# Scores and gathers one step further ahead in a talking-heads attention kernel, with a fourth gather buffer, against a first batch loaded all at once

## Chip, core and metric

One core of a Trainium2 chip runs the whole program in one launch. The metric is the device time of that launch in microseconds: 2410.34 us as the median of three runs (2408.38 to 2414.39). Everything is computed in 32-bit floats.

Five engines work beside each other, each in its own program order: TensorE (in the profile PE, and PEld for its weight loads), VectorE (DVE), ScalarE (ACT), GpSimd (POOL) and SyncE (SP). SyncE only issues transfers here, GpSimd issues some and computes, ScalarE issues transfers only at the start.

## What is computed

```python
# q, k, v: (8, 12, 448, 64); w_pre, w_post: (12, 12)
scores = (1 / sqrt(64)) * q @ k.T                      # per batch and head
scores = einsum('bhij,hg->bgij', scores, w_pre)        # heads are mixed before ...
attn = softmax(scores, axis=-1)                        # (with 1e-9 in the sum)
attn = einsum('bhij,hg->bgij', attn, w_post)           # ... and after the softmax
x = (attn @ v) as (8, 448, 768)
u = x + real(fft(fft(x, axis=1), axis=2))
un = (u - mean) / sqrt(var + 1e-6)
out = u + relu(un @ w_ch1) @ w_ch2                     # w_ch1: 768 x 3072, w_ch2: 3072 x 768
```

## The kernel before

**Attention** runs in 192 steps, 24 to a batch (`GS`), three to a block of score rows (`BS`), six to a group (`GT`). For a block, `emit_qk` computes the scores of all twelve heads (three pairs of pairs, `xx`) and ScalarE copies them from PSUM to `Sb`. Mixing heads is a matmul over heads, so heads have to lie in partitions: `emit_gather` moves a step's rows of `Sb` into `Kr`, with four transfers from SyncE. Then come, each for one step: premix (matmul by `w_pre`), maximum (VectorE), exponential (ScalarE), scaling (GpSimd), postmix (matmul by `w_post`), and a transpose on VectorE (`emit_turn`) that brings keys into partitions for attention times V (`emit_av`).

```python
    pkr = pool("pkr", 3)
    ppp = pool("ppp", 3)
    psm = pool("psm", 4)
    ...
    def emit_qk(n, xx):
        bk = blocks[n]
        st = batches[bk["b"]]
        if "Sb" not in bk:
            bk["Sb"] = psb.tile([P, 6, S], F32, name="Sb", tag="Sb")
        ...                                  # 16 matmuls into two PSUM tiles
        return [lambda x=x: copy(ENG["QK"][x], bk["Sb"][:124, 2 * xx + x, :],
                                 pss[x][:124, :S]) for x in range(2)]

    def emit_gather(T):
        Kr = pkr.tile([P, 2, S], F32, name="Kr", tag="Kr")
        Sb = blocks[T // BS]["Sb"]
        row = _row(Sb)
        for z in range(2):
            for x in range(2):
                p0 = MG + 4 * (T % BS) + 2 * z + x
                nc.sync.dma_start(
                    out=Kr[64 * x:64 * x + KR, z, :],
                    in_=_ap(Sb, p0 * row, [[RS * row, 2 * R], [S, 6], [1, S]]))
        steps[T]["Kr"] = Kr
    ...
        def done(y):                         # of emit_av
            for e in range(2):
                ...
                copy(ENG["AV"][y], dst, src)     # XT <- PSUM, 128 x 60
```

The order of work in a step is a list, one for even and one for odd steps; what is due in which step stands in tables. `LG` is how many steps a gather stands ahead of its postmix, `LM` how many the premix.

```python
AT_QK = ((1, 2, 2), (0, 1, 2), (0, 1, 2), (1, 1, 2),
         (0, 1, 2), (0, 1, 2), (0, 1, 2), (0, 1, 2))
ORDERS = tuple(o.split() for o in (
    "conv pre post flush AV max0 exp0 "
    "QK max1 exp1 turn scale full gather",
    "pre post flush max0 max1 QK exp0 "
    "AV turn exp1 scale gather conv full flush"))
    ...
    LG, LM = 4, 2
    ...
        for n in range(0 if b else 2, 2 * NG):
            for xx in range(3):
                due("QK", f + BS * n - 7 + AT_QK[n][xx],
                    lambda n=2 * NG * b + n, xx=xx: (emit_qk(n, xx), n))
    ...
        while s <= TOT - GS + AT_X[-1]:
            ...
            for op in ORDERS[s % 2]:
                if op == "flush":
                    flush()                  # pending copies out of PSUM
                elif op in fill:
                    take(op, s)              # what is due: QK, AV, transposes, Z, S2
                elif op == "conv":
                    if s >= 4:
                        wts.deal(1)          # one VectorE operation of the weights
                elif op == "gather":
                    if 0 <= s + LG < TOT:
                        if any(e[2] is not None and e[2] <= (s + LG) // BS for e in pend):
                            flush()
                        emit_gather(s + LG)
                ...                          # pre, max, exp, scale for s + LM; post, turn for s
```

**The first batch** has a path of its own: its q and k are all loaded at once, on SyncE and ScalarE, the last pair into a buffer of `Pv` that is free then; the scores of its first two blocks follow at once. All other batches load on GpSimd, step by step, into four raw buffers.

```python
        if y == 0 and b == 0 and xx == START[-1]:
            if "raw" not in first:
                first["raw"] = ppv.tile([P, GT, 2 * S], F32, name="Pv", tag="Pv")
            ...
            eng = nc.gpsimd if b else (nc.sync, nc.scalar)[x]
```

**Weights** come as 64-bit floats. VectorE turns every piece into 32 bits in seven operations (`begin` to `whole`), and four sums of pieces are formed besides, so that the network's products need fewer matmuls. `deal` hands out these operations, one a step in attention, two to four at a time in the network. Each piece and each sum is stored to memory from GpSimd; each has a buffer of its own (`slot`) but for the sum that goes onto piece 6.

```python
        def new(slot):
            box[slot] = self.pst.tile([P, DH], F32, name="wst", tag=f"wst{slot}")[:, :w]
            return box[slot]
        def store(slot):
            self.later.append(lambda: nc.gpsimd.dma_start(out=dst[slot], in_=box[slot]))
        ...
        def total(o, a, op, b):
            to = box[o] if o == 6 else new(o)
            vec.tensor_tensor(to, box[a], box[b], op=op)
            store(o)
```

**The network** (`ffn_phase`) follows: 42 rounds of seven products with `w_ch1` and seven with `w_ch2`, on TensorE nearly without a gap.

## Time and profile before

| stage | from, to (us) | PE busy | DVE busy | ACT busy | POOL busy |
|---|---|---|---|---|---|
| start, to the first turned step | 0 to 41.8 | 23.89 | 11.16 | 15.50 | 9.38 |
| attention, 100 us of it | 200 to 300 | 99.71 | 86.81 | 71.61 | 78.72 |
| attention, 100 us of it | 500 to 600 | 95.74 | 87.40 | 67.69 | 73.24 |
| passage to the network | 800 to 860 | 53.33 | 39.71 | 29.84 | 33.93 |
| network, 500 us of it | 1300 to 1800 | 500.00 | 281.32 | 57.58 | 60.26 |

The span is 2408.6 us with 54664 instructions. How the lines of a profile are read: a group has its line of the kernel, engine, operation, what it writes and reads, and a count; then busy time in us, mean ns of one, and the idle time of the engine just before it with what ended it. A wait reads "engine line <- who ended it: us in total, times, longest". A row of windows gives, after the length, busy us and count of each engine, then the granted clock of TensorE as a share of full speed, the busy share of the transfer engines, and GB/s. Starts of matmuls are recorded; their ends are modelled, so busy time of PE is more than its work.

### The profile page before, as it was taken

To read this page: it belongs to the slowest core of one execution; us is meant where nothing else is said; L and a number is where in the kernel's file an instruction comes from. 1 tells how busy PE (TensorE), PEld (TensorE's weight loads), DVE (VectorE), ACT (ScalarE), POOL (GpSimd) and SP (SyncE) were. 2 spreads that over 40 slices of the span, in tenths; PEclk is the share of its full clock that TensorE was granted. 3 is DMA by queue.
4 is the path that set the end of the run, shared out by engine and by line. 5 is a ranking of instruction groups with operands and counts; after the bars stand their busy time and mean duration, and the time that the engine had idled before them with its cause. 6 is when DMAs were issued, how large, how long until landed. Compare 5 with 4: busy or idle time off the path is not lost.

```text
span 2408.6 us, 54664 instructions
## 1 busy us (share of the span) xinstructions
PE 2361.9 (98%) x21680; PEld 1596.2 (66%) x21680; DVE 1543.8 (64%) x3139; ACT 798.8 (33%) x2055; POOL 787.3 (33%) x1255
## 2 busy tenths in 40 slices
PE   6999999999999999999999999999999999999999
PEld 2555555555555577677777777777777777777776
DVE  3888988888897767775656356635664457433333
ACT  4776777666667632221110110110110110111110
POOL 3597877868776541211111011101110011000000
PEclk9999999999999999999999999999999999999999
DMA  7565555655554566437444444544442644353331
GB/s 161 161 182 165 185 171 165 193 161 178 170 171 157 165 237 191 154 116 254 136 146 139 151 151 125 158 132 156 143 157 93 197 135 140 120 170 113 117 118 53
DMA packets 169100, 372.50 MB, mean 155 GB/s; under 512 B 36750, under 2 KB 90790, under 8 KB 168846
## 3 DMA queue, kind: packets, MB, share of 16 engines
q1 hardware_dynamic: 129902, 261.60, 33.1%
q0 software_dynamic: 33376, 106.03, 15.3%
q8 instruction: 173, 2.83, 0.5%
q10 hardware_dynamic: 5568, 1.38, 0.4%
q14 instruction: 81, 0.66, 0.1%
HBM read 211.98 MB, written 74.34 MB: 119 GB/s over the span
## 4 chain that ended last, share of the span: by engine, by line
PE 91%; DMA 3%; DVE 2%; ACT 1%; SPq 1%; POOL 1%; issue 1%; ACTq 0%; DVEq 0%; POOLq 0%
PE psP L980 18%; PE psP L1036 18%; PE psR L980 9%; PE psR L1036 9%; PE mx L486 7%; PE ms L459 5%; PE ms L547 5%; PE po L520 5%; PE psQ L1036 5%; PE psQ L980 5%; DMA Kr<-Sb 2%; PE ms L661 2%; PE ms L434 1%; PE ms L645 1%; SPq L475 1%; PE ms L580 1%
## 5 line engine op out<-in xcount | busy, mean ns | idle before, releaser
L980 PE MATMUL psP<-ub,w1t 128*128 128x256 f32 x2016 | 462.5, 379 | 0.0
L1036 PE MATMUL psP<-w2t,h 128*128 128x384 f32 x1344 | 460.9, 486 | 0.0
L980 PEld LDWEIGHTS psP<-ub,w1t 128*128 128x128 f32 x2016 | 382.8, 190 | 60.7
L213 POOL DMA_DIRECT2D raw<-in_moe_w_ch_dram x120 | 68.6, 571 | 919.4 <-DVE tmp L257 908.5
L1036 PEld LDWEIGHTS psP<-w2t,h 128*128 128x128 f32 x1344 | 254.4, 190 | 165.9
L510 POOL TENSOR_SCALAR PP<-PP,rcp 128x448 f32<-128x448 f32 x384 | 253.6, 670 | 228.2 <-DVE rcp L508 199.3
L500 ACT ACTIVATE PP<-mx,nmx 128x448 f32<-128x448 f32 x384 | 240.7, 632 | 172.3 <-DVE nmx L493 158.5
L493 DVE TENSOR_REDUCE nmx<-mx 128x1 f32<-128x448 f32 x384 | 222.7, 616 | 94.1 <-PE mx L486 91.9
L985 ACT COPY h<-psP 128x512 f32<-128x512 f32 x42 | 24.6, 586 | 764.7 <-PE psP L980 753.6
L1042 DVE TENSOR_TENSOR u<-u,psP 128x384 f32<-128x384 f32 x336 | 183.4, 552 | 141.4 <-PE psP L1036 139.2
L486 PE MATMUL mx<-Kr,kw 60*32 60x448 f32 x3072 | 236.4, 552 | 16.7 <-DMA Kr<-Sb 11.7
L980 PE MATMUL psR<-ub,w1t 128*128 128x256 f32 x1008 | 231.3, 379 | 0.0
L1036 PE MATMUL psR<-w2t,h 128*128 128x384 f32 x672 | 230.5, 486 | 0.0
L991 DVE TENSOR_TENSOR h<-h,psQ 128x512 f32<-128x512 f32 x42 | 28.9, 688 | 298.8 <-PE psQ L980 298.8
L520 PE MATMUL po<-PP,kw 60*32 60x448 f32 x3072 | 215.5, 541 | 4.9 <-DVE rcp L507 2.4
L531 DVE STREAM_TRANSPOSE Pv<-po 128x896 f32<-128x896 f32 x192 | 212.4, 1106 | 9.3 <-PE po L520 6.2
L459 PE MATMUL ms<-kT,qT 64*32 64x448 f32 (+1 forms) x3072 | 207.6, 545 | 7.4 <-ACT qT L330 6.4
L980 PEld LDWEIGHTS psR<-ub,w1t 128*128 128x128 f32 x1008 | 191.4, 190 | 25.9
L330 ACT COPY Sb<-ms 124x448 f32<-124x448 f32 x384 | 184.0, 542 | 33.8 <-DMA Kr<-Sb 17.4
L547 PEld LDWEIGHTS ms<-Pv,vv 64*64 64x64 f32 x5376 | 145.4, 134 | 70.5 <-issue 35.2
L1036 PEld LDWEIGHTS psR<-w2t,h 128*128 128x128 f32 x672 | 127.2, 190 | 87.4
L547 PE MATMUL ms<-Pv,vv 64*64 64x120 f32 x5376 | 168.6, 270 | 1.2 <-issue 1.2
(95 smaller groups left out, 2813.9 us busy)
## 6 DMA issues: line engine op xcount, KB each, us to landing
ub<-ub SPq DMA_DIRECT2D x294, 384.0 KB
Kr<-Sb SPq DMA_DIRECT2D x768, 105.0 KB
raw<-in_moe_w_ch_dram POOLq DMA_DIRECT2D x72, 256.0 KB, 3.6
raw<-in_moe_w_ch_dram POOLq DMA_DIRECT2D x48, 384.0 KB, 3.6
w<-wst POOLq DMA_DIRECT2D x126, 128.0 KB, 3.3
w<-wst POOLq DMA_DIRECT2D x84, 192.0 KB, 2.6
w1t<-w SPq DMA_DIRECT2D x42, 384.0 KB
w2t<-w SPq DMA_DIRECT2D x42, 384.0 KB
```

Of the source, the lines that this page charges most:

```text
L330: (nc.scalar.copy if eng == "a" else nc.vector.tensor_copy)(out=out, in_=in_)
L459: nc.tensor.matmul(pss[x][o:o + hi - lo, :S], st["qT", xx][64 * x:64 * x + 64, y, lo:hi], st["kT", xx][64 * x:64 * x + 64, y, :], start=Tr ...
L486: nc.tensor.matmul(mx[x][64 * z + o:64 * z + o + 32, :S], kw1[64 * x:64 * x + KR, o:o + 32], Kr[64 * x:64 * x + KR, z, :], start=True, sto ...
L493: nc.vector.tensor_reduce(nmx[:, :], steps[T]["mx"][x][:, :S], axis=AX.X, op=ALU.max, negate=True)
L500: nc.scalar.activation(steps[T]["PP"][:, x, :], steps[T]["mx"][x][:, :S], ACTF.Exp, bias=steps[T]["nmx", x][:, :], accum_out=steps[T]["den ...
L510: nc.gpsimd.tensor_scalar(PP[:, x, :], PP[:, x, :], rcp[:, x:x + 1], 1.0, op0=ALU.mult, op1=ALU.mult)
L520: nc.tensor.matmul(po[o:o + 32, z, :S], kw2[64 * z:64 * z + KR, y, :], PP[64 * z:64 * z + KR, :, c * HS:(c + 1) * HS], start=True, stop=True)
L531: nc.vector.transpose(g["Pv"][:, T % GT, :].rearrange("p (z s) -> p z s", z=2), steps[T]["po"][:, :, :S])
L547: nc.tensor.matmul(pss[y][64 * x:64 * x + 64, :nu * R], st["v", pr][64 * y:64 * y + 64, x, jb * D:(jb + 1) * D], _ap(Pv, 64 * y * rp + 32 ...
L980: nc.tensor.matmul(p[:, m, :], w1[i][:, kc, m * P:(m + 1) * P], ub[:, kc, :], start=i in OPENS and m == kc == 0, stop=kc == NK - 1, skip_g ...
L1036: nc.tensor.matmul(p, lhs[i][:, kf, x * P:(x + 1) * P], w2[i][:, kf, :], start=i in OPENS and kf == 0, stop=kf == FM - 1, skip_group_check ...
L1042: nc.vector.tensor_tensor(us_, us_, p, op=ALU.add)
```

## The change

What it does, in the order of weight:
- Scores and gathers go one step further ahead (`LG` 4 to 5, scores at −8 in place of −7), with a fourth buffer for `Kr`. It is for the premix to find its rows landed.
- To make room, `psm` has three buffers in place of four, `XT` is two columns narrower, and the weights' sums are written over pieces that are no longer needed, so that five staging buffers do in place of seven.
- The tables of what is due when, the two orders in a step and the choice of engine for some copies are new: half the copies of attention times V go to VectorE, and the smaller copy of k goes from VectorE to ScalarE.
- The first batch's own path is gone: its loads, transposes and scores follow the same tables as those of the other batches.

```diff

-XW = GR + 12
+XW = GR + 10
 ...
-AT_T = ((6, 10), (17, 18), (14, 16))
+AT_T = ((4, 11), (17, 16), (14, 14))
 AT_L = ((-4, -3), (-2, -1), (0, 1), (2, 8), (12, 13), (14, 15))
 AT_V = ((3, 4), (5, 6), (7, 7))
-AT_QK = ((1, 2, 2), (0, 1, 2), (0, 1, 2), (1, 1, 2),
-         (0, 1, 2), (0, 1, 2), (0, 1, 2), (0, 1, 2))
-AT_AV = ((1, 2, 3), (0, 1, 5), (3, 4, 5), (1, 2, 4))
-AT_X = (11, 20, 24, 29)
-AT_Z = (39, 39, 41, 41)
+AT_QK = ((0, 2, 3), (0, 1, 2), (1, 2, 3), (1, 1, 2),
+         (0, 1, 2), (0, 1, 2), (0, 0, 2), (0, 0, 2))
+AT_AV = ((1, 2, 3), (0, 1, 5), (3, 4, 5), (1, 3, 5))
+AT_X = (11, 20, 24, 30)
+AT_Z = (39, 39, 41, 42)
 AT_S = ((40, 44), (48, 54))
 
 ORDERS = tuple(o.split() for o in (
-    "conv pre post flush AV max0 exp0 "
-    "QK max1 exp1 turn scale full gather",
-    "pre post flush max0 max1 QK exp0 "
-    "AV turn exp1 scale gather conv full flush"))
+    "pre post max0 max1 exp0 AV QK "
+    "gather conv exp1 turn scale full flush",
+    "pre post max0 exp0 max1 turn exp1 "
+    "AV QK gather full flush scale conv"))
 
 ENG = {("tr", "q", 4): "d", ("tr", "q", 3): "a", ("tr", "k", 4): "a",
-       ("tr", "k", 3): "d", "QK": "aa", "AV": "aa", "X": "aa", "z": "a"}
+       ("tr", "k", 3): "a", "QK": "aa", "AV": "da", "X": "aa", "z": "a"}
 ...
-            sums = ((4, 6, ALU.add, 3), (5, 4, ALU.subtract, 0),
-                    (6, 0, ALU.subtract, 6), (2, 1, ALU.subtract, 5))
 ...
         def new(slot):
-            box[slot] = self.pst.tile([P, DH], F32, name="wst", tag=f"wst{slot}")[:, :w]
+            tag = {0: 0, 6: 1, 1: 2, 2: 3, 3: 3, 4: 4}[slot]
+            box[slot] = self.pst.tile([P, DH], F32, name="wst", tag=f"wst{tag}")[:, :w]
             return box[slot]
 ...
         def total(o, a, op, b):
-            to = box[o] if o == 6 else new(o)
-            vec.tensor_tensor(to, box[a], box[b], op=op)
+
+
+            if o == 4:
+                new(o)
+            elif o != 6:
+                box[o] = box[1 if o != 5 else 2 if 2 in box else 0]
+            vec.tensor_tensor(box[o], box[a], box[b], op=op)
             store(o)
 ...
-    pkr = pool("pkr", 3)
+    pkr = pool("pkr", 4)
     ppp = pool("ppp", 3)
-    psm = pool("psm", 4)
+    psm = pool("psm", 3)
 ...
-    first = {}
-    START = sorted(range(3), key=lambda xx: max(AT_T[xx]))
 ...
-        if y == 0 and b == 0 and xx == START[-1]:
-
-            if "raw" not in first:
-                first["raw"] = ppv.tile([P, GT, 2 * S], F32, name="Pv", tag="Pv")
-            batches[b]["raw" + nm, xx] = first["raw"][:, nm == "q"].rearrange(
-                "p (c x d) -> p c x d", c=C7, x=2)
-        elif y == 0:
+        if y == 0:
 ...
-        (nc.gpsimd if b else nc.sync).dma_start(
+        nc.gpsimd.dma_start(
 ...
-    LG, LM = 4, 2
+    LG, LM = 5, 2
 ...
+    loads = []
     for b in range(B):
         f = b * GS
         at_t = [(a, nm, xx) for xx, at in enumerate(AT_T) for nm, a in zip("qk", at)]
-        if b == 0:
-
-            for i, xx in enumerate(START):
-                for j, nm in enumerate("kq"):
-                    for y in range(2):
-                        due("none", -40, lambda xx=xx, nm=nm, y=y: emit_load_qk(0, xx, nm, y))
-                    due("full", 2 * i + j - 20, lambda xx=xx, nm=nm: emit_xpose(0, xx, nm))
-                for n in range(2):
-                    due("QK", 2 * i + 2 + n - 20, lambda n=n, xx=xx: (emit_qk(n, xx), n))
-            for pr in range(3):
-                for y in range(2):
-                    due("none", -40, lambda pr=pr, y=y: emit_load_v(0, pr, y))
-        else:
-            for at, (a, nm, xx) in zip(AT_L, sorted(at_t, key=lambda e: e[0])):
-                for y in range(2):
-                    due("none", f + at[y] - GS,
-                        lambda b=b, xx=xx, nm=nm, y=y: emit_load_qk(b, xx, nm, y))
-            for xx, at in enumerate(AT_T):
-                for nm, a in zip("qk", at):
-                    due("full", f + a - GS,
-                        lambda b=b, xx=xx, nm=nm: emit_xpose(b, xx, nm))
-        for pr in range(3 if b else 0):
+        for at, (a, nm, xx) in zip(AT_L, sorted(at_t, key=lambda e: e[0])):
+            loads.append(f + a - GS)
+            for y in range(2):
+                due("none", f + at[y] - GS,
+                    lambda b=b, xx=xx, nm=nm, y=y: emit_load_qk(b, xx, nm, y))
+        for xx, at in enumerate(AT_T):
+            for nm, a in zip("qk", at):
+                due("full", f + a - GS, lambda b=b, xx=xx, nm=nm: emit_xpose(b, xx, nm))
+        for pr in range(3):
             for y in range(2):
                 due("none", f + AT_V[pr][y], lambda b=b, pr=pr, y=y: emit_load_v(b, pr, y))
-        for n in range(0 if b else 2, 2 * NG):
+        for n in range(2 * NG):
             for xx in range(3):
-                due("QK", f + BS * n - 7 + AT_QK[n][xx],
+                due("QK", f + BS * n - 8 + AT_QK[n][xx],
                     lambda n=2 * NG * b + n, xx=xx: (emit_qk(n, xx), n))
 ...
-    due("none", -39, emit_load_mix)
+    due("none", max(loads[:6]) - 6, emit_load_mix)
```

## The prediction

> **What bounds the kernel now.** I read the page first: shares of busy time (part 1), then the chain that ended last (part 4).
>
> ```profile
> PE 2361.9 (98%) x21680; PEld 1596.2 (66%) x21680; DVE 1543.8 (64%) x3139; ACT 798.8 (33%) x2055; POOL 787.3 (33%) x1255
> ...
> PE 91%; DMA 3%; DVE 2%; ACT 1%; SPq 1%; POOL 1%; issue 1%; ACTq 0%; DVEq 0%; POOLq 0%
> PE psP L980 18%; PE psP L1036 18%; PE psR L980 9%; PE psR L1036 9%; PE mx L486 7%; PE ms L459 5%; PE ms L547 5%; PE po L520 5%; PE psQ L1036 5%; PE psQ L980 5%; DMA Kr<-Sb 2%; PE ms L661 2%; PE ms L434 1%; PE ms L645 1%; SPq L475 1%; PE ms L580 1%
> ```
>
> TensorE carries 91% of the chain. L980 and L1036, the feed-forward network from about 845 us on, make up 64% of it; the change hardly touches them. The only sizable piece that is no TensorE work is `DMA Kr<-Sb`, the gather: 2%, some 58 us by the list of the chain (2.4%). That is a ceiling: it counts latencies that other work may hide.
>
> The trace has one transpose `Pv<-po` (L531) per attention step: the first at 41.8 us, the last, the 192nd, at 836.2. Every 24th begins a batch. The busy times of four of the eight batches, cut there (PE, PEld, DVE, ACT, POOL, then granted clock):
>
> ```profile
> 136.60:235.00 98.40, 97.61 (x1954) 52.55 (x1938) 82.52 (x164) 71.37 (x211) 79.86 (x124) 1.00 0.58 173
> 435.90:539.50 103.60, 101.20 (x1951) 57.09 (x1949) 87.72 (x172) 71.48 (x211) 79.71 (x122) 0.98 0.58 174
> 539.50:646.70 107.20, 101.51 (x1962) 57.21 (x1954) 92.03 (x172) 71.52 (x211) 82.98 (x126) 0.98 0.57 174
> 748.00:836.00 88.00, 84.52 (x1699) 46.60 (x1695) 67.52 (x141) 57.31 (x178) 48.79 (x73) 1.00 0.47 153
> ```
>
> Equal work takes 98.4 us in batch 1 and 107.2 in batch 5. The eight are 94.8, 98.4, 99.4, 101.5, 103.6, 107.2, 101.3, 88.0. To see what TensorE needs at least, I took from the trace the time from the first start of a group of matmuls to the first start of the next group, medians: premix 0.776 (24 per batch), postmix 0.752 (24), scores 0.890 (24), attention times V 1.64 (12), transposes of X 0.84 (4), of q and k 0.914 (6), Z 1.725 per two (2), S2 1.402 (4). Sum: 18.6 + 18.0 + 21.4 + 19.7 + 3.4 + 5.5 + 3.5 + 5.6 = 95.7 us. Batches 1 to 6 exceed it by 2.7, 3.7, 5.8, 7.9, 11.5 and 5.6: 37 us. Batch 0 (few AV, no Z) and 7 (no loads, fewer scores) have perhaps 14 and 4 more. So about 55 us is all that attention could give back.
>
> Who holds TensorE up there? The table of waits up to 850 us (total, times, longest):
>
> ```profile
> PEld mx L486 <- DMA Kr<-Sb: 33.5, 43, 4.0
> ...
> PE mx L486 <- DMA Kr<-Sb: 11.7, 8, 3.2
> ...
> ACT Sb L330 <- DMA Kr<-Sb: 17.4, 12, 3.2
> ```
>
> The gather leads. From 60 to 840 us alone it is 25.9 us at the weight load, 5.0 at the matmul. The true loss lies between these, since the matmul's end is modelled. The worst case in the timeline:
>
> ```profile
> 546.19 10.98 SPq L475 DMA_DIRECT2D Kr<-Sb  x12
> ...
> 552.32 1.05 PE L486 MATMUL mx<-Kr,kw 60*32 60x448 f32 x12
> ...
> 556.43 0.57 PE L486 MATMUL mx<-Kr,kw 60*32 60x448 f32 x2 [3.07 <-DMA Kr<-Sb]
> ```
>
> Twelve gathers, three steps' worth, leave back to back at one per 0.81 to 0.92 us. The second step's last one leaves near 552.5 and lands by 556.4, so the premix stops for 3.07 us. Then the clock drops:
>
> ```profile
> 558.30:561.70 3.40, 3.40 (x71) 2.56 (x71) 1.24 (x4) 1.11 (x6) 1.85 (x3) 0.50 0.68 169
> ```
>
> [...] clock 0.50 for 3.4 us at 496.8 and 558.3, each after a gather stall; such a window costs up to half its length, 1.7 us. [...] Our gathers go by SyncE[...]: about 3.9 us from issue to landing above. So a further step of lead covers them more surely than faster issue would. [...]
>
> **The change part by part.**
>
> *Gather and scores a step earlier.* `LG` 4 to 5, scores at −8 in place of −7, `Kr` with 4 buffers. Each gather leaves one step before (3.99 us = 95.7/24), while its distance to the scores and to the release of its buffer is unchanged: the buffer of `T` was freed by the premix of `T−3`, now of `T−4`, again emitted one step ahead of the gather. Slack grows by about 4.0 us, above the longest wait (3.2 us at the matmul, 4.0 at the weight load). From 60 us on nearly all gather waits should go: between 5.0 and 25.9 us, I take 13; two half-clock windows, 3 us; the premixes run in two halves because half their rows had come, and the delayed exponentials behind them, 4 us. Gain 20 us.
>
> *Orders and tables.* AV now comes ahead of the scores in both orders, `conv` after the gather in even steps. The order cannot remove work from TensorE. I give it 3 us of the remaining 17 (37−20).
>
> *Engines.* Rows between 60 and 840 us:
>
> ```profile
> L330 ACT COPY XT<-ms 128x60 f32<-128x60 f32 x368 | 68.2, 211 | 36.3 <-PE ms L547 26.7 <-PE po L520 3.5
> ...
> L406 POOL DMA_DIRECT2D rawk<-in_k_dram x78 | 57.2, 734 | 0.0
> ...
> L330 DVE COPY kT<-ms 128x384 f32<-128x384 f32 x21 | 11.4, 542 | 0.0
> ```
>
> Half the copies of `XT` go to VectorE: 8 × 4 × 3 × 2 = 192. With ScalarE's 0.211 us as an estimate of one, +40 us for VectorE, less 24 × 0.542 = 13 us for the `kT` copies that leave it: +27 us over attention, 3.4 a batch. It is busy 82.5 to 92.0 us a batch now, so 86 to 95 against TensorE's 95.7. ScalarE is relieved by 40 − 13 = 27 us. I charge 3 us for VectorE coming late.
>
> *First batch as all others.* Its loads leave on GpSimd: 24 × 0.734 = 17.6 us from about 1.6 us, so the last leaves near 19 and lands 4 to 5 us later, near 23.5 (median landing in the steady state 4.2 to 5.2 us). Transpose and copy take 1.9 us (24.63 to 26.54 now), then scores of pair 1 and pair 2 with about 1 us of copy each: first gather near 28.5. Now it leaves at 28.61, held by the serial transposes and copies from 15.3 on, not by the loads; V's loads no longer precede those of the mixing weights. So nothing lost by this reckoning; with copies on ScalarE alone and GpSimd's waits I charge 2 us. From there SyncE issues a step's gathers in 3.3 us, and the start stays bound by that.
>
> *Sums in place.* The same VectorE instructions, two tags fewer. A sum over a piece waits for that piece's store, in flight since the deal before; in the network each deal is 2.6 us apart and TensorE is ahead of nothing it needs. 0 us. The extra step after the last (`AT_X` 30): +1 us.
>
> Sum: −20 −3 +3 +2 +0 +1 = −17; with some credit for a second-order effect (a stall that is gone no longer delays the next block's scores), −20: 2390 us.
>
> **Rivals.**
> 1. *The gather wait gives way to VectorE.* For it: VectorE up to 95 us a batch against TensorE's 95.7, and on the worst stall an L249 instruction of 2.77 us (mean 0.637) delayed the maximum until 556.30. Against: its waits at `nmx` for the premix were 92 us, so it has air. It would leave 2400 to 2415.
> 2. *SyncE cannot use the extra buffer.* A step's gathers need 4 × 0.81 = 3.25 us of 3.99, and one store waits there for an indirect DMA (15.2 us in 6 waits). Scores cannot overwrite `Sb` until its gathers have landed; that distance is not changed, so ScalarE's 17.4 us of waiting may stay. For it: SyncE's own waits are mostly for ScalarE (`Sb`, 52.4 us in 25 waits), not for a free `Kr`. Then half the gain: about 2400.
> 3. *The retuned schedule takes nearly all.* All six middle batches at 96.5 us: 611.4 − 579 = 32 us, and 4 in batch 0: about 2374.
> 4. *The start gets longer.* If GpSimd's loads, with four raw buffers, reach the first gather only at 36 us, 8 us of the gain go: about 2400.
>
> **Range and chances.** TensorE's floor in the network makes 2355 the least thinkable (all 55 us). Rivals 1, 2 and 4 lead to 2400 to 2415, rival 3 to 2374. Eight in ten: 2370 to 2416. Faster by 2% needs less than 2362.1, that is 48 of 55 us: 0.06. Slower by 2%, over 2458.5, needs a new stall in every batch or in the network: 0.02. Within: 0.92.
>
> **What would show it.** `DMA Kr<-Sb` falls from 2.4% of the chain below 1%; its weight-load wait between 60 and 840 us from 25.9 to under 8; no half-clock window between 60 and 830 us; batches 1 to 6 between 96.5 and 100; the first `Pv<-po` within 3 us of 41.8; the network's stretch unchanged within 3 us. I am wrong if VectorE waits (`nmx`, `rcp`, `po`) grow at TensorE as gather waits fall, if the first `Pv<-po` is beyond 48 us, or if the network gets longer through stores of sums.

## The result, and the profile after

The changed kernel takes 2438.53 us (median of 4, 2433.03 to 2444.50) beside 2410.46 us for the kernel before on the same chip: ratio 1.0115, 95% interval 1.0088 to 1.0142. It is slower by 28 us; the prediction was 2390, and its range ended at 2416.

The page after, busy times, then the chain of work that ended last by engine and by line:

```profile
PE 2361.9 (97%) x21680; PEld 1589.7 (65%) x21680; DVE 1551.4 (64%) x3307; ACT 779.3 (32%) x1887; POOL 784.6 (32%) x1261
...
PE 89%; DMA 3%; DVE 2%; POOL 2%; SPq 2%; ACT 1%; issue 1%; ACTq 0%; DVEq 0%; POOLq 0%
PE psP L1022 18%; PE psP L966 18%; PE psR L966 9%; PE psR L1022 9%; PE ms L545 6%; PE mx L484 5%; PE ms L457 5%; PE po L518 5%; PE psQ L1022 5%; PE psQ L966 4%; DMA Kr<-Sb 2%; PE ms L659 2%; SPq L473 2%; PE ms L432 1%; PE ms L643 1%
```

TensorE's busy time is the same to a tenth, yet its share of the chain fell from 91 to 89%. GpSimd (POOL) and SyncE's queue (SPq) have the points. The gather, `DMA Kr<-Sb`, still has its 2%: what the change was made for didn't come.

Cut at the starts of the transposes `Pv<-po`, as in the prediction, the two profiled executions differ so:

| stage (us) | before | after | difference |
|---|---|---|---|
| to the first `Pv<-po` | 41.8 | 44.5 | +2.7 |
| batch 0 | 94.9 | 94.3 | −0.6 |
| batches 1 to 6 | 611.3 | 615.4 | +4.1 |
| batch 7, to the last `Pv<-po` | 88.2 | 101.3 | +13.1 |
| to the network's first `psP` | 17.3 | 17.0 | −0.3 |
| first `psP` to the first product of the second layer ("passage") | 23.1 | 31.9 | +8.8 |
| the rest of the network | 1531.9 | 1532.0 | +0.1 |

A later profile of the unchanged kernel before (below, e16) had 605.2 in batches 1 to 6, so a difference of 6 us in that row is within what two executions of one program show; there the passage was 23.1 and the network 1531.9 again. Two places stand out to which the prediction gave nothing and 1 us: the last batch and the passage.

**Steady part.** Batches 1, 4 and 7, cut as in the prediction, each with PE, PEld, DVE, ACT, POOL, then the granted clock:

```profile
138.80:239.90 101.10, 96.31 (x1940) 52.05 (x1939) 83.36 (x185) 69.14 (x191) 79.61 (x124) 1.00 0.57 171
443.10:548.50 105.40, 100.37 (x1959) 56.66 (x1958) 87.28 (x192) 69.06 (x191) 80.59 (x124) 0.98 0.59 172
...
754.20:855.40 101.20, 87.16 (x1676) 46.45 (x1672) 72.83 (x164) 55.69 (x158) 55.48 (x84) 0.95 0.47 151
```

VectorE is at 83 to 87 us of a full batch (89.6 in batch 5), below TensorE's 96 to 100, so by its busy time it isn't the bound; what its order of work does is shown at e3. The table of waits between 60 and 840 us:

```profile
PEld ms L545 <- ACT Sb L336: 35.9, 44, 3.5
ACT Sb L336 <- DMA Kr<-Sb: 33.8, 12, 4.8
...
PEld mx L484 <- DMA Kr<-Sb: 16.9, 14, 3.6
...
PE mx L484 <- DMA Kr<-Sb: 8.9, 5, 2.8
```

The gather waits at the premix are fewer at the weight load (14 for 37, 16.9 us for 25.9) and longer at the matmul (5 as before, but 8.9 us for 5.0), and a new wait leads: attention times V (`ms L545`), now ahead of the scores, waits for PSUM that ScalarE's copies to `Sb` free. SyncE, between 60 and 815 us:

```profile
SPq L473 <- ACT Sb L336: 109.4, 34, 8.7
```

Before it was 52.4 us, as the prediction noted. SyncE stands longer because the last scores come no earlier, as one stall shows (timeline of SyncE, then of TensorE):

```profile
238.59 19.64 SPq L473 DMA_DIRECT2D Kr<-Sb  x16
...
252.85 0.95 PE L484 MATMUL mx<-Kr,kw 60*32 60x448 f32 x12
256.63 0.57 PE L484 MATMUL mx<-Kr,kw 60*32 60x448 f32 x2 [2.84 <-DMA Kr<-Sb]
```

SyncE had its place in the order long before, waited from 241.04 to 246.66 us for the last `Sb` copy (246.63), and then sent this step's four gathers, the last at 249.09, with seven more close behind. By its semaphore that last one landed at 256.59, 7.5 us after its issue; the premix had stopped for 2.84 us.

**Last batch.** VectorE, GpSimd and TensorE, where the network's first statistics meet attention's last steps:

```profile
831.73 0.56 DVE L908 BATCH_NORM_STATS2 st<-u 128x6 f32<-128x384 f32 x1 [4.75 <-DMA u<-v]
...
848.61 1.94 POOL L599 TENSOR_TENSOR xs<-X 113x384 f32<-113x384 f32 x2
...
852.27 1.26 POOL L508 TENSOR_SCALAR PP<-PP,rcp 128x448 f32<-128x448 f32 x2
...
833.45 1.75 PE L518 MATMUL po<-PP,kw 60*32 60x448 f32 x16 [4.56 <-DVE rcp L505]
...
853.59 1.75 PE L518 MATMUL po<-PP,kw 60*32 60x448 f32 x16 [5.49 <-POOL PP L508]
```

In VectorE's order the network's first statistic (L908) stands ahead of a transpose and a reciprocal of attention and waits 4.75 us for a load of `u`; postmix waits with it. Later GpSimd works through the normalisation and the folds (L599) before attention's last scaling (L508), and postmix waits 5.49 us more. Within each pause the granted clock falls to 0.50, and it stays there for 6.83 us (the third window belongs to the passage, next):

```profile
831.60:838.40 6.80, 4.87 (x48) 1.29 (x48) 6.31 (x15) 1.96 (x6) 2.50 (x4) 0.50 0.58 156
852.10:858.90 6.80, 5.31 (x74) 3.55 (x75) 1.56 (x3) 0.42 (x2) 6.37 (x10) 0.50 0.58 180
879.40:886.20 6.80, 4.02 (x13) 3.36 (x14) 2.85 (x8) 0.54 (x1) 5.26 (x8) 0.50 0.97 314
```

**Passage.** Z and S2 are products of the Fourier transform; ahead of Z, GpSimd folds its input to `xf`. TensorE, first after, then before:

```profile
872.47 2.75 PE L966 MATMUL psP<-ub,w1t 128*128 128x256 f32 x12
881.92 0.69 PE L643 MATMUL ms<-ts,xf 113*97 113x113 f32 x2 [6.70 <-POOL xf L620]
```

```profile
853.53 2.75 PE L980 MATMUL psP<-ub,w1t 128*128 128x256 f32 x12
856.12 1.47 PE L661 MATMUL ms<-tcs,z 96*113 96x193 f32 x8
...
865.20 0.94 PE L645 MATMUL ms<-ts,xf 113*97 113x113 f32 x8
```

Before, the first of attention's remainders between the network's products is an S2 (L661), and Z (L645) comes 9 us later, when GpSimd's folds `xf` are just done. After, Z comes first and waits 6.70 us.

### The profile page after: what moved, and what is told of

Same layout as the page of the kernel before. It is cut to its first block, busy times and chain, and to the rows that moved or that the text cites. A ratio compares the mean times of both kernels' runs of the same rounds, so it can differ in the third digit from the quotient of the medians.

```text
span 2436.4 us, 54562 instructions
## 1 busy us (share of the span) xinstructions
PE 2361.9 (97%) x21680; PEld 1589.7 (65%) x21680; DVE 1551.4 (64%) x3307; ACT 779.3 (32%) x1887; POOL 784.6 (32%) x1261
## 4 chain that ended last, share of the span: by engine, by line
PE 89%; DMA 3%; DVE 2%; POOL 2%; SPq 2%; ACT 1%; issue 1%; ACTq 0%; DVEq 0%; POOLq 0%
PE psP L1022 18%; PE psP L966 18%; PE psR L966 9%; PE psR L1022 9%; PE ms L545 6%; PE mx L484 5%; PE ms L457 5%; PE po L518 5%; PE psQ L1022 5%; PE psQ L966 4%; DMA Kr<-Sb 2%; PE ms L659 2%; SPq L473 2%; PE ms L432 1%; PE ms L643 1%
## 5 line engine op out<-in xcount | busy, mean ns | idle before, releaser
L508 POOL TENSOR_SCALAR PP<-PP,rcp 128x448 f32<-128x448 f32 x384 | 245.9, 650 | 236.0 <-DVE rcp L506 193.2
L484 PE MATMUL mx<-Kr,kw 60*32 60x448 f32 x3072 | 218.7, 550 | 17.3 <-DMA Kr<-Sb 14.8
L518 PE MATMUL po<-PP,kw 60*32 60x448 f32 x3072 | 207.1, 547 | 15.2 <-DVE rcp L505 6.9
L545 PEld LDWEIGHTS ms<-Pv,vv 64*64 64x64 f32 x5376 | 146.4, 133 | 83.8 <-issue 39.3
L457 PE MATMUL ms<-kT,qT 64*32 64x448 f32 (+1 forms) x3072 | 198.0, 553 | 2.5 <-ACT Sb L336 1.6
L545 PE MATMUL ms<-Pv,vv 64*64 64x120 f32 x5376 | 172.8, 269 | 10.1 <-ACT Sb L336 6.2
```

What stands on the lines that cost most here:

```text
L457: nc.tensor.matmul(pss[x][o:o + hi - lo, :S], st["qT", xx][64 * x:64 * x + 64, y, lo:hi], st["kT", xx][64 * x:64 * x + 64, y, :], start=Tr ...
L484: nc.tensor.matmul(mx[x][64 * z + o:64 * z + o + 32, :S], kw1[64 * x:64 * x + KR, o:o + 32], Kr[64 * x:64 * x + KR, z, :], start=True, sto ...
L508: nc.gpsimd.tensor_scalar(PP[:, x, :], PP[:, x, :], rcp[:, x:x + 1], 1.0, op0=ALU.mult, op1=ALU.mult)
L518: nc.tensor.matmul(po[o:o + 32, z, :S], kw2[64 * z:64 * z + KR, y, :], PP[64 * z:64 * z + KR, :, c * HS:(c + 1) * HS], start=True, stop=True)
L545: nc.tensor.matmul(pss[y][64 * x:64 * x + 64, :nu * R], st["v", pr][64 * y:64 * y + 64, x, jb * D:(jb + 1) * D], _ap(Pv, 64 * y * rp + 32 ...
```

## Experiments

Ratios are to the kernel before, run on the same chip; before's own median was 2402 to 2407 us on these. "Mended" names the parts that the diffs show.

**e1, e2: the network's first operations held in program order.** In both kernels the first statistic and the first normalisation step may no longer move ahead of attention's last operations.

```diff
+            if t == x == y == 0:
+                tc.keep_in_program_order(bn)      # nc.vector.bn_stats(...)
 ...
+        if t == 0:
+            tc.keep_in_program_order(pw)          # nc.gpsimd.tensor_scalar(var, ...)
```

> The changed kernel, but the network's first VectorE instruction (the statistics of the first tokens) and its first GpSimd instruction are held behind all attention work on their engines. Theory P (passage): in the changed kernel these two stand ahead of the last attention steps on in-order engines, wait for a load of u (4.75 us) and hold up a postmix (5.5 us), and the clock halves three times after it [...]. Then the time falls from 2438.5 to 2418 to 2428, the last batch from 101 to under 93 us, and batches 1 to 6 stay at 615 us. Rival S (the loss is in the steady attention steps): the time stays within 4 us of 2438.

> The kernel before with the same two instructions held back. Theory P: there they cost only 1.4 and 2.4 us of waiting, so holding them back is worth little: 2405 to 2414 us. If holding them back were a gain of its own, whatever the schedule, it would be 2395 or less; then e1 would say nothing of the change.

Measured: 1.0140 (1.0119 to 1.0160) and 1.0024 (1.0013 to 1.0036). In the changed kernel the last batch fell from 101.3 to 89.7 us, so its stalls do come from those operations' place. But then the statistics start at 861.9 us, and TensorE waits for the normalised rows:

```profile
PE psQ L937 <- ACT un L928: 9.3, 1, 9.3
```

From the last `Pv<-po` to the first `psP` it took 29.0 us in place of 17.0, and the passage grew to 37.8 us. The place of the statistics is a trade; holding them back gains nothing, and in the kernel before it costs 6 us.

**e3: lead on the kernel before.** Lead, scores at −8, four gather buffers, sums in place, the new table of transposes; first batch, orders, score table and engines of before.

```diff
-    pkr = pool("pkr", 3)
+    pkr = pool("pkr", 4)
 ...
-    LG, LM = 4, 2
+    LG, LM = 5, 2
 ...
-                due("QK", f + BS * n - 7 + AT_QK[n][xx],
+                due("QK", f + BS * n - 8 + AT_QK[n][xx],
```

> The kernel before with only the lead: gathers and scores one step ahead, fourth gather buffer (made room for by the sums in place, as in the changed kernel), and the table of the transposes of q and k of the changed kernel, which the earlier scores need; orders, engines, other tables and the first batch's path stay. Every block's scores are a step earlier here. Theory L (the lead works where all blocks have it, and the orders or the score table undo it in the changed kernel): batches 1 to 6 take 585 to 602 us in place of 611, time 2390 to 2403 (five steps stand behind the first statistics, which may cost up to 5 us more). Rival Q (SyncE issues 3.25 us a step and the copies of scores wait for gathers, so an extra buffer moves the wait and removes nothing): batches 1 to 6 at 606 to 620 us, time 2408 to 2425.

Measured: 1.0067 (1.0047 to 1.0088). The gather waits are gone, and the kernel is slower all the same, with 619.1 us in batches 1 to 6: TensorE's gaps ahead of a premix that follows scores are 16.5 us (before 2.0), and the wait of the premix's weight load for ScalarE's exponentials (46 to 742 us) is

```profile
PEld mx L492 <- ACT PP L506: 47.5, 74, 4.6
```

against 16.1 us before. ScalarE often only passes a wait on. In the longest of these waits a sum of weights stands ahead of the maxima in VectorE's order, waits for a store and takes 3.09 us; the exponential waits for its maximum, and the premix for the exponential:

```profile
587.07 3.09 DVE L273 TENSOR_TENSOR wst<-wst 128x384 f32<-128x384 f32 x1 [0.73 <-DMA w<-wst]
...
590.09 1.14 DVE L499 TENSOR_REDUCE nmx<-mx 128x1 f32<-128x448 f32 x2
590.79 0.63 ACT L506 ACTIVATE PP<-mx,nmx 128x448 f32<-128x448 f32 x1 [4.58 <-DVE nmx L499]
...
591.57 0.97 PE L492 MATMUL mx<-Kr,kw 60*32 60x448 f32 x4 [3.81 <-ACT PP L506]
```

Followed back in this way through the trace, 39.4 of the premix's 57.9 us of waits for exponentials (weight load and matmul, 46 to 742 us) go to exponentials that had waited for a maximum; for 19.8 us of them the maximum came directly behind an operation of the weights, for 13.5 us behind the clearing of `XT`, which waits for ScalarE's copies. In e10, below, it is 25.6 of 38.6 us. No run has the lead without the sums in place and with four `psm` buffers, so their part in the cost of the lead isn't separated.

**e4: the score table.** A last entry of 3 at −8 puts a block's last scores at −5, where a 2 at −7 had put them before; and −5 is now the gather's own step. So blocks 0 and 2 of every eight got no lead.

```diff
-AT_QK = ((0, 2, 3), (0, 1, 2), (1, 2, 3), (1, 1, 2),
+AT_QK = ((0, 2, 2), (0, 1, 2), (0, 1, 2), (1, 1, 2),
```

> The changed kernel with the score table's blocks 0 and 2 at (0,2,2) and (0,1,2) in place of (0,2,3) and (1,2,3): in the changed kernel the last score of these two blocks is due in the step of their gather, as late as before, so that they have no lead at all. Theory G (that is why gather waits stayed): the weight load's wait for gathers between 60 and 815 us falls from 16.9 to under 8 us, batches 1 to 6 from 615 to 603 to 609, time 2426 to 2434. Rival Q: no change beyond 3 us in either.

Measured: 1.0059 (1.0039 to 1.0079), 0.0056 below the changed kernel's ratio: 13 us, by the two intervals 5 to 22. Batches 1 to 6 took 604.3 us in place of 615.4, the premix's gather wait left the table, and SyncE's wait for `Sb` fell:

```profile
SPq L473 <- ACT Sb L336: 60.4, 38, 3.0
```

Of the parts put back one at a time, this is the only one whose return shows in the time.

From the traces, the time from the fourth gather issue of a block's first step to its premix, medians over batches 1 to 6, by block of the batch:

| block | 0 | 1 | 2 | 3 | 4 | 5 | 6 | 7 |
|---|---|---|---|---|---|---|---|---|
| before | 4.5 | 4.9 | 3.7 | 4.6 | 5.5 | 3.9 | 5.9 | 7.4 |
| after | 5.3 | 7.2 | 3.8 | 9.5 | 10.7 | 6.8 | 8.7 | 10.3 |
| e4 | 9.0 | 9.7 | 8.8 | 8.8 | 11.2 | 6.9 | 8.6 | 11.8 |
| e14, new orders alone | 4.5 | 4.9 | 2.6 | 4.2 | 0.4 | 3.6 | 4.4 | 7.4 |

The lead is there in all blocks of the changed kernel but 0 and 2. Block 2 is the one that stalls: between 60 and 840 us it has all 8.9 us of the matmul's waits for gathers and 14.3 of the 16.9 us at the weight load; block 0, with 5.3 us of distance, has 1.4. Measured from its issue to the last update of its semaphore, a gather takes 3.9 us in the median of the changed kernel (3.4 before), but more than 6 us in 109 of 733 cases (before 96), so 3.8 us of distance is too little.

**e5: the last slot.**

```diff
-AT_X = (11, 20, 24, 30)
+AT_X = (11, 20, 24, 29)
```

> The changed kernel with the last product of AT_X at 29 again in place of 30, so that attention's loop ends one step earlier. Theory 'one slot too few': the step added at the end does the last S2 inside the loop, so that the parts of the normalisation that are interleaved with the network's first products start with Z one slot (about 7.8 us) earlier, before GpSimd's folds are ready; TensorE then waits 6.7 us for the fold. By it this run has from the last psP ahead of the normalisation to the first product of the second layer about 23 to 25 us in place of 31.9 (before 23.1), no wait of Z for the fold above 2 us, and 2429 to 2434 us, 5 to 9 less than the changed kernel's 2438.5. Rival 'GpSimd late': the folds themselves come later in the changed kernel, because the statistics start after more of attention's work on GpSimd; then the passage stays above 30 us and the time at 2436 to 2441.

Measured: 1.0130 (1.0083 to 1.0176). The mechanism is confirmed: the passage is 23.1 us, and Z comes when its fold is there, behind an S2.

```profile
889.07 1.47 PE L659 MATMUL ms<-tcs,z 96*113 96x193 f32 x8
...
898.15 0.94 PE L643 MATMUL ms<-ts,xf 113*97 113x113 f32 x8
```

But the time didn't fall by what the passage gave. That entry of `AT_X` moves work in every batch, not only in the last, and batches 1 to 6 took 627.9 us in this profile, which shows the slowest of the run's four executions (2444.0 us, median 2436.0). The interval is wide, yet it has hardly room for a gain of 8.8 us; where that went isn't settled.

**e6, e7, e9: orders, first batch, engines of the kernel before, each alone in the changed kernel.** e6 puts back `ORDERS`, e7 the first batch's path, e9 the table `ENG`:

```diff
-       ("tr", "k", 3): "a", "QK": "aa", "AV": "da", "X": "aa", "z": "a"}
+       ("tr", "k", 3): "d", "QK": "aa", "AV": "aa", "X": "aa", "z": "a"}
```

> The changed kernel with the two ORDERS of the kernel before (in even steps the attention products behind postmix and ahead of the scores, the scores late; in odd steps the scores ahead of the attention products, which stand behind the maxima). Theory 'the order costs': with the attention products ahead of the scores in odd steps they wait for PSUM that ScalarE's score copies free (35.9 us in 44 waits), and this is what keeps batches 1 to 6 at 615 us; by it that wait falls below 18 us and batches 1 to 6 to 600 to 608 us, time 2426 to 2432. Rival 'only the scores' place in the table': with the scores behind their table place anyway, the order changes which engine is waited for and not how long; batches 1 to 6 at 612 to 620 us, time 2434 to 2443. Either way the last batch and the passage into the network stay long (b7 97 to 102 us, passage 30 to 33 us), unless the orders are what puts the network's first statistics ahead of attention's last turns.

> The changed kernel with the first batch's own path of the kernel before put back: all loads of q and k at once, the third head pair's in the two halves of a V buffer, transposes and first scores in that order ahead of the loop, V's loads on SyncE; lead and tables otherwise as changed. Theory 'the common path costs the start': the first Pv<-po comes at 41.5 to 43.0 us in place of 44.5 and the time falls by 1.5 to 3 us, to 2435 to 2437. Rival 'the lead costs the start': with scores and gathers a step earlier two steps' gathers must leave ahead of the first premix whatever the loads do (the kernel before with the lead alone began at 45.3); then the first Pv<-po stays at 44 to 46 and the time at 2437 to 2441.

> The changed kernel with the engine table of the kernel before (copies of XT all on ScalarE, kT copies of the third chunk on VectorE). Theory 'the engines cause the last batch's stalls': with a third of the XT copies on VectorE, VectorE runs behind in the last batch, the network's first statistics and GpSimd's power and folds slip in ahead of attention's last scale, and postmix waits 4.6 + 5.5 us for them, each wait followed by half clock. With the old table the last scale on GpSimd stands ahead of the network's again: last batch 88 to 93 us in place of 101.3, no wait of postmix above 3 us there, and 2426 to 2431. Rival 'the engines are neutral at the end, the lead does it' : last batch 97 to 102, time 2435 to 2441. In the steady part the scores' table still rules: batches 1 to 6 at 610 to 620.

Measured: 1.0148 (1.0099 to 1.0198), 1.0137 (1.0091 to 1.0182), 1.0113 (1.0086 to 1.0139), none to be told from 1.0115. For the orders the wait of attention times V for `Sb` copies fell from 35.9 to 16.6 us, and the premix's for exponentials rose from 22.5 to 32.7 (60 to 840 us); batches 1 to 6 took 622.9 us, more than either theory expected. For the first batch, the first `Pv<-po` came at 42.6 in place of 44.5. For the engines, GpSimd's last scaling stood ahead of the network's operations again, and its wait vanished; what VectorE's early statistic costs stayed:

```profile
PE po L518 <- DVE rcp L505: 4.3, 2, 3.4
```

The last batch took 96.0 us in place of 101.3, between the two forecasts, and batches 1 to 6 took 623.9. But e6, with the new engine table and the old orders, has no such wait for GpSimd either, while e4, e5, e7 and e8, which have both tables new, all have it (5.5 us). So the GpSimd stall needs the new engine table and the new orders together, and its end doesn't show in the time. (The table moves half of the copies of `XT` to VectorE, not a third.)

**e8, e10, e11: mended together.** e8 has e4, e5 and e7; e10 has the engines of e9 besides; e11 has also the third block's scores of the first batch at −7.

> The changed kernel with three of its parts mended: the score table of the fourth run (no block's last score in its gather's own step), the last AT_X at 29, and the first batch's own path of the kernel before. If the three causes are apart and add up: 2438.5 - 17.5 (scores) - 7 (slot) - 2 (start) = 2412, within 2408 to 2416, no different from the kernel before (ratio 0.999 to 1.003); what is left above it is the last batch (97 us in place of 88). If they overlap (a stall that is gone is taken up by the next): 2417 to 2421. If the lead really pays once nothing is in its way: below 2405.

> The eighth run (score table mended, last AT_X at 29, first batch's own path) with the engine table of the kernel before as well; of the change it keeps lead, four gather buffers, orders, attention tables and sums in place. If the engine table is what is left of the loss: last batch 88 to 91 in place of 98.1, batches 1 to 6 at 600 to 607, passage about 23, time 9 us less than the eighth run's 2416, that is 2404 to 2409 or 0.999 to 1.003 of the kernel before. If ScalarE, with 192 more copies of XT, now comes late for the exponentials: batches 1 to 6 at 610 to 618 and 2412 to 2418.

> The run above, and in the first batch the third block's scores one step later (-7 in place of -8), so that the first two premixes stand next to each other again, as in the kernel before; in the eighth run scores of the third block stood between them and the third premix then waited 3.3 us for the exponentials. Expected: first Pv<-po at 41.8 to 43 in place of 45.6, the time 2 to 3.5 us below the run above: 2401 to 2406, at or just below the kernel before (ratio 0.997 to 1.001). If the start only moves and the first batch gives it back (it took 89.1 us there, 94.9 before): no difference to the run above.

Measured: 1.0051 (1.0035 to 1.0066), 1.0048 (1.0036 to 1.0060), 1.0046 (1.0030 to 1.0062). Beyond the score table nothing adds up: 13 us came from e4, and 2 to 3 from all that followed, within the intervals. e11 moved the first `Pv<-po` from 44.8 to 42.9, and batch 0 gave back more than that (97.7 for 90.6). All stay 11 to 12 us above the kernel before, although the gather waits at the premix are gone.

**e12: sums in place alone**, on the kernel before.

> The kernel before with the weights' sums in the place of stored pieces and nothing else. The prediction gave it 0 us. Theory 'free': 2408 to 2412 at a before of 2410, ratio 0.999 to 1.001. Rival 'a sum holds VectorE': an in-place sum must wait for its piece's store, and stands ahead of a maximum in VectorE's order (in the third run one waited 0.73 us, took 3.09 and held the premix 3.8 us); then VectorE waits of L273 for the store appear in several batches and the time is 3 to 10 us more, ratio 1.001 to 1.004.

Measured: 0.9999 (0.9983 to 1.0016). On the kernel before, the sums in place are free, within 4 us.

**e13 to e18: lead and orders apart.** e13 is e10 with the lead taken back, e15 is e10 with the old orders, e18 with neither; e14 is the kernel before with the new orders alone, e17 is e3 with the new orders.

```diff
-    LG, LM = 5, 2                                       # e13, e18
+    LG, LM = 4, 2
 ...
-                due("QK", f + BS * n - 8 + AT_QK[n][xx],
+                due("QK", f + BS * n - 7 + AT_QK[n][xx],
 ...
-    "pre post max0 max1 exp0 AV QK "                    # e15, e18; the other way in e14, e17
+    "conv pre post flush AV max0 exp0 "
 ...
```

> The tenth run with the lead alone taken back: LG 4 and scores at -7, all else of it kept (orders, attention tables and sums in place of the changed kernel; engines, first batch, last AT_X and score table mended). If the lead pays in a kernel in which nothing is in its way, this run is 5 to 12 us slower than the tenth run's 2415 (2420 to 2427), with the premix's weight-load wait for gathers back at 20 to 30 us in attention. Rival 'the lead only exchanges waits' (the tenth run lost 3 us between halves of the premix in place of 14, and 16 in place of 5 ahead of premix and postmix, where ScalarE's exponentials and copies are late): then this run is within 4 us of the tenth, 2411 to 2419. If the lead itself costs (one block of scores more ahead of the first premix, the network's statistics called before their data at the end): 2403 to 2410.

> The kernel before with the two ORDERS of the changed kernel and nothing else. Prediction's term for it: -3 us. If the orders cost by themselves (attention products ahead of the scores in odd steps wait for PSUM that ScalarE's score copies free): a wait of ms for ACT Sb of 25 to 40 us at the weight load of the attention products, where the kernel before has none, and 2408 to 2418 beside a before of about 2403 (ratio 1.002 to 1.006). If they are neutral: ratio 0.999 to 1.001. If they help: below 0.999.

> The tenth run with the ORDERS of the kernel before. If the new orders are what keeps the mended kernel 12 us above the kernel before: 2403 to 2409, the wait of the attention products for ACT Sb (32.6 us) below 8 us. If the new orders are made for the lead and help it (the third run, with the lead on the kernel before and its old orders, was at 1.0067): 2418 to 2424, with waits of premix for ACT PP of 45 us or more at the weight load in place of 36.6.

> The kernel before, unchanged, profiled on the same chip as the three above, to see how far the same program's stages differ between executions. Expected: network stretch within 0.3 us of 1531.9, passage within 0.3 of 23.1, batches 1 to 6 together within 8 us of 611.3, first Pv<-po within 1.5 us of 41.8. If batches 1 to 6 differ by more than 8 us, differences of single traces below that say nothing by themselves.

> The third run (kernel before with lead, fourth gather buffer, sums in place and the new table of transposes) with the ORDERS of the changed kernel as well: the fourth corner beside before (1.000), orders alone (1.012) and lead alone (1.0067). If the two costs add: 1.019, 2449 beside a before of 2403. If orders and lead need each other (the new orders put the scores behind the attention products, so gathers leave later, and the lead pays for that): 0.999 to 1.006, gather waits gone, premix's waits for ACT PP below the third run's 47 us at the weight load, batches 1 to 6 at 603 to 610. Below 0.998 it would be a version that beats both kernels.

> The tenth run without lead and without the new orders: what is left of the change is its tables of attention products, Z and transposes, the scores' places in the mended table, the sums in place and the buffers. If the tables cost nothing by themselves: ratio 0.999 to 1.003, and the tenth run's 1.0048 is what lead and orders together cost. If the tables are what keeps the tenth run above the kernel before: 1.005 to 1.012, with batches 1 to 6 at 612 to 620 us.

Measured, as ratios with their intervals. The lead runs of the first row have sums in place, three `psm` buffers and the new transposes too. In e16, the unchanged kernel, the first `Pv<-po` came at 41.5, batches 1 to 6 took 605.2 and the passage 23.1, so only differences beyond some 6 us in batches 1 to 6 count:

| | old orders, no lead | new orders, no lead | old orders, lead | new orders, lead |
|---|---|---|---|---|
| tables of before | 1 | e14 1.0120 (1.0091 to 1.0150) | e3 1.0067 (1.0047 to 1.0088) | e17 1.0055 (1.0035 to 1.0075) |
| mended tables | e18 1.0105 (1.0079 to 1.0132) | e13 1.0239 (1.0218 to 1.0260) | e15 1.0114 (1.0090 to 1.0138) | e10 1.0048 (1.0036 to 1.0060) |

In their profiles, batches 1 to 6 took 605.2 (e16), 629.1, 619.1 and 612.3 us in the upper row, 635.3, 639.4, 632.6 and 607.0 us in the lower. e13 is slower than any of its three forecasts.

The costs don't add. In the upper row they would make 1.019, and it is 1.0055. In the lower row the lead alone changes nothing (e18 to e15), the orders alone cost 0.013 (e18 to e13), and the lead under the new orders is worth 0.019, 46 us (e13 to e10). The new orders put the scores behind attention times V in odd steps too; without the lead the gathers then come late (0.4 us ahead of the premix in block 4 of e14), and TensorE waits for them (46 to 742 us; before 8.2 and 30.3):

```profile
PE mx L486 <- DMA Kr<-Sb: 23.0, 19, 3.7
...
PEld mx L486 <- DMA Kr<-Sb: 49.0, 55, 4.5
```

In the upper row the lead pays back a good half of what the orders owe. In the lower row it pays back more: lead and orders together are 0.0057, 14 us, below the same tables without either (e10 against e18). So with those tables the pair does pay, but only about half of the 0.0105 that the tables cost. The prediction took orders and tables together, as a gain of 3 us. In e10 the same two rows of waits are replaced by others:

```profile
PE ms L651 <- ACT Sb L336: 4.1, 6, 0.8
PE ms L440 <- ACT Sb L336: 3.2, 4, 1.3
PE mx L492 <- ACT PP L506: 2.0, 4, 0.8
...
PE mx L492 <- DMA Kr<-Sb: 1.0, 3, 0.5
...
PEld mx L492 <- ACT PP L506: 36.6, 78, 1.6
PEld ms L553 <- ACT Sb L336: 32.6, 44, 1.7
```

To see it as lost time, I summed from the traces what successive matmul starts lie apart beyond 0.38 us (a 448-column pass: two take 0.752 us in postmix, 0.776 in premix, by the medians in the prediction), where it is over 0.40, from 30 to 840 us, by what came before and after:

| gaps (us) | all | premix to premix | scores to premix | premix to postmix | postmix to AV |
|---|---|---|---|---|---|
| before | 42.4 | 14.1 | 2.0 | 3.1 | 4.1 |
| before again (e16) | 44.8 | 15.8 | 2.1 | 2.4 | 4.5 |
| after | 62.4 | 18.3 | 1.8 | 11.5 | 14.3 |
| lead alone (e3) | 50.8 | 3.0 | 16.5 | 4.7 | 4.6 |
| lead and orders (e17) | 46.4 | 3.1 | 8.3 | 5.9 | 8.0 |
| mended (e10) | 53.0 | 3.1 | 7.7 | 8.0 | 8.9 |

The lead takes 11 to 13 us out of the gaps between a premix's halves, wherever it is whole, and the other three columns take as much or more. (The stretch ends at 840 us in all rows, so a slower kernel has a little less of its last batch in it.) No corner of the square beats the kernel before.

## Why the prediction was wrong

**"Each gather leaves one step before … its distance to the scores … is unchanged"** is the step that failed first. I checked `LG` and the −8 and didn't add the table: 3 at −8 is 2 at −7. Two of eight blocks had no lead, and block 2 kept the stalls; that cost 13 us (e4), and the gather kept its 2% of the chain (1% in e4).

**"From 60 us on nearly all gather waits should go … Gain 20 us"** failed a second time where the lead was whole. The waits went (e3, e4, e10, e17), but the gain didn't come: 16 us slower in e3, and 14 us slower in e4 at 1.0059. The prediction took the gather's 13 us, its clock windows and the delayed exponentials as time that nobody else would claim. TensorE's next wait, for ScalarE's exponentials and its copies out of PSUM, stood close behind: 57.9 us for exponentials alone in e3, where it was 17.4 before. By the traces most of it is handed on from VectorE's maxima; that is read from single executions, and no run changed VectorE's order to show it. The reading of the worst stall was wrong as well. The gather that ended it is the last of the first of the three steps, not of the second: issued at 548.62, landed at 556.39, so it took 7.8 us and not 3.9. The half-clock windows at 496.8 and 558.3 us, which I counted as 3 us, are absent from the second profile of the same kernel (e16, with a mean granted clock of 0.997 in place of 0.996); they were that execution's own.

**"The order cannot remove work from TensorE. I give it 3 us"**: alone the orders cost 29 us (e14). The sentence is true of work and says nothing of waits. An order decides how late the scores are, and through them the gathers.

**Engines, +3 us**: 0 within the interval in e9 (1.0113) and in e10 against e8. So the moved copies aren't what the kernel lost; but rival 1, that the gather wait gives way to VectorE, is not out by that. Its sign, a growing wait of TensorE for VectorE, appears in e3 under another name, as a wait for ScalarE. What the engine table did do, together with the orders, is put the network's GpSimd operations ahead of attention's last scaling, which no row of the steady part could tell.

**First batch, +2 us**: 2.7 us measured at the first `Pv<-po`, but from a wrong reading. I had all its loads leave on GpSimd; q and k still leave on SyncE and ScalarE, and only V's moved. Nor is the path the only cause: e3, e8 and e10 have the old path and the whole lead, and begin at 45.3, 45.6 and 44.8 us, so the lead by itself costs 2 to 3 us there (e12 and e13, with the old path and no lead, begin at 42.9 and 41.8). Bringing the start back won nothing in e7 and e11.

**Sums in place, 0**: right on the kernel before (e12); with the lead a sum held the maxima in e3, so there it stays open.

**"The extra step … +1 us"**: 8.8 us of passage. The step itself is cheap. It used up an S2 that was filling TensorE while GpSimd folded, so Z came one slot early and waited 6.70 us.

**Left out of the sum**: the last batch, +13.1 us. I looked at the attention's middle and at the network and took the seam for constant.

The signs I had named: the chain's gather share under 1% (it is 2.5; two profiles of the kernel before have 2.4 and 3.2), the weight-load wait under 8 us (16.9), no half-clock window between 60 and 830 us (514.2 and 565.4, 3.4 us each), batches 1 to 6 between 96.5 and 100 (100.1 to 105.4) all came out wrong; the first `Pv<-po` within 3 us (+2.7) and the network within 3 us (+0.1) right. Rival 2 was nearest for the changed kernel: SyncE's waits are for `Sb`, and I had written that down with its number, and then given it half the gain. For the kernels with the whole lead rival 1 is nearer.

What stays open is why the new tables alone cost 0.0105. In e18 all 68.9 us of the premix's waits for exponentials go back to exponentials that had waited for a maximum, but no run put the tables back one by one:

```profile
PE mx L492 <- ACT PP L506: 20.6, 14, 3.8
...
PEld mx L492 <- ACT PP L506: 48.3, 56, 4.6
```

Open too is where the mended kernels still lose their 12 us. In the trace of e10, one of its faster executions (2410.6 us, median 2414.9), batches 1 to 6 take 607.0 us, no more than before; its last batch takes 94.6, some 6 us more.

## What to carry to other kernels

When a pipeline stage is moved ahead, add the offset to every entry of the table that feeds it; a stage has the lead of its latest input, and here two blocks of eight decided. A wait that ends last in a tuned kernel has others close behind it, so its removal is worth at most the distance to the next one, and lead, order and tables tuned together have to be judged together: here each alone cost 16 to 29 us, and both together 13. When a wait is put down to an engine, ask what that engine had waited for in its turn. Look at the seams between phases, where operations of the next phase stand in the same engine's order: 22 of the 28 us between the two traces stood there, though mending one seam alone won no time that shows.

## What the runs showed of the hardware

In the profiles of the kernel before and of the changed one the granted clock of TensorE is 1.00 or 0.50. From 60 to 900 us the windows at 0.50 are 3.41 us long at 496.8, 558.3 and 841.6 before; in the changed kernel they are 3.41 us long at 514.2 and 565.4, and 6.83 us at 831.6, 852.1 and 879.4. These last five starts lie 51.2, 266.2, 20.5 and 27.3 us apart, close to 15, 78, 6 and 8 times 3.41. TensorE's pauses at the windows, as the profile models the ends of its matmuls, differ widely: before, 496.8 followed pauses of 0.46 and 1.02 us, and 558.3 one of 3.07; in the changed kernel it is 2.49 and 2.45 us at the two short windows, and 4.56, 5.49 and 6.70 at the three long ones. A pause of 2.84 us, up to 256.63, had none: the clock was 1.00 from 250 to 262 us. So which pauses bring a window isn't shown here. Over the three long windows TensorE was busy for 14.20 of 20.40 us, all at a clock of 0.50.

The stages of one program repeat unevenly: the network to 0.1 us (1531.9 in both profiles of before), batches 1 to 6 only to 6 us (611.3 and 605.2), so a few us in attention can be read from repeated times and not from one trace.
